# One top-k attention with two squared-ReLU FFNs: the last output weight is converted before the second input weight, one-tile units take two 128-blocks, and the order is written anew

## The chip, the cores and the metric

The kernel runs on one core of a Trainium2 chip. The metric is the device time of one execution in microseconds (us): the kernel before takes 1159.86 us, the median of three runs. TensorE is called PE here, VectorE DVE, ScalarE ACT, GpSimd POOL, and SyncE, which issues all the DMAs, SP.

## The reference

```python
scores = (q @ k.T) / sqrt(64)                 # 4 batches, 8 heads, 576 x 576
kth    = 32nd largest score of each row
attn   = softmax of the scores >= kth, 0 elsewhere
x      = (attn @ v), heads side by side       # 2304 tokens x 512
x      = (s * relu(x @ w_in)**2 + b) @ w_out        # moe: 512 -> 2048 -> 512
out    = relu(x @ w2_in)**2 @ w2_out                # moe2: 512 -> 2048 -> 512
```

The four weights arrive as 64-bit floats, which the kernel reads as pairs of 32-bit words; the rest is f32.

## The kernel before

**Tiles and units.** The 2304 tokens are 18 tiles of 128 rows. For each tile and head PE forms the scores into a PSUM bank pair `pS` (L599), DVE finds the 32nd largest in four rounds of `max` (L610) and three of `match_replace` (L621) and masks the exponentials (L652 or L658), ACT makes the exponential (L624) and its fp16 high half (L654 or L661), POOL the fp16 low half (L456, called from L673), a DMA transposes both into `pT` (L675), and PE multiplies by V into `pA` (L685). Eight heads make a tile of x; `finish_x` and `split_x` scale it, split it in two fp16 halves and transpose it by DMA into `xT` (L706).

**The FFNs.** `ffn(u, which)` runs a unit of one or two tiles through 16 blocks of 128 hidden columns. Per block: 12 matmuls into a PSUM bank (`f_in`, L788), a ReLU on ACT (L797), two squares on ACT (fp16 `gh`, L799, and f32 `gg`, L802), the low half `gl` on POOL (L807), then three matmuls per tile into `pC` (`f_out`, L834). The first FFN has units of one tile for tiles 0 to 10 and for tile 17, and three pairs; the second has one-tile units for tiles 0 and 17 and eight pairs. In one-tile units most blocks alternate between the banks `pH` and `pC[1]`; in pairs a block of 256 rows always uses `pH`. Before a second-FFN unit can start it needs its x in `xT[2]` or `xT[3]`, written by the end of the first FFN (`ffn1_end`, which adds the column sums `bcs`).

**The weights.** There are four, in 16 pieces each, numbered W0 (`moe_w_in`), W1 (`moe_w_out`), W2 (`moe2_w_in`), W3 (`moe2_w_out`). `pieces` loads a piece of 512 KB as pairs of words into a raw buffer, `to_f32` turns it into f32, `gram` takes its squared column norms on PE, `weight_scale` makes a power of two, and `split_w` makes two fp16 halves. Way D of `to_f32` uses three DVE operations (L919, L928, L935); way T gives the second to ACT (L924) and POOL (L456). Way P of `split_w` forms the low half on PE (two f32 passes L957 and one fp16 matmul L958, then a copy on ACT, L961); way O scales and rounds on ACT (L947, L948) and subtracts on POOL (L456). W0, W1 and W2 stay on chip (`w1`, `wo1`, `w2`). W3 is written back to DRAM as `wo2` (stores on SP) and streamed through the two `wring` buffers in each second-FFN unit. W0 and W1 use five raw buffers, W2 and W3 three; converted pieces of W3 wait in six f32 places, their halves in two staging tiles.

**The order.** Every operation is given to a planner (`Plan`) with a duration, a priority and the tiles it reads and writes; program order sets the dependences. `order()` simulates five engines and the DMA queue with these durations and with the delays of `WAIT`, picks by priority (`prio` plus an offset from the table `TW` by tag and by step), and its result is the fixed order in which each engine's instructions are emitted. An engine's instructions then run in that order whatever their real durations are. Before, the program order of the weights is W0, W1, the column sums (L1092), W2, W3.

Of the kernel before, what the change touches and what calls it, by code (L numbers as in the profile page):

```python
# [8 lines left out]
F32 = mybir.dt.float32  # L9
# [21 lines left out]
O2P = 10  # L31
O2S = 14
GROUPS = (1, 1, 4, 4)
CONV = ('DT', 'T', 'D', 'T')
SPLIT = ('P', 'P', 'O', 'P')
# [31 lines left out]
WKT = 2  # L67
# [45 lines left out]
}  # L113

WAIT = {("dve", "dve"): 0.127, ("act", "act"): 0.2, ("pool", "pool"): 0.1, ("pe", "pe"): 0.0, ("sp", "sp"): 0.0,
# [5 lines left out]
COLD, COLD_T = 1.35, 260.0  # L121
AVOID = 0.1
DMA_F, LAND, DRAIN = 1.3, 1.25, True
# [8 lines left out]
class Plan:  # L132
# [33 lines left out]
    def order(self):  # L166
# [27 lines left out]
        while len(out) < n:  # L194
# [59 lines left out]
            if kinds[i] == 2:  # L254
                end = max(end, queue if DRAIN else mine)
                queue = mine = (end if DRAIN else max(end, queue)) + lat
                done = queue + LAND
            elif kinds[i] == 1:
                queue = max(end + 0.65, queue) + lat * DMA_F
                if e == "sp":  # L260
                    mine = queue
                done = queue + LAND
# [21 lines left out]
def kernel(  # L284
# [81 lines left out]
    wraw += [(xT[i].rearrange("p a b -> p (a b)").bitcast(I32), [f"xT{i}_0", f"xT{i}_1"]) for i in range(3)]  # L366
# [200 lines left out]
    def attention(t, h, prio):  # L567
# [39 lines left out]
        for rd in range(TOPK // 8):  # L607
# [39 lines left out]
        else:  # L647
# [3 lines left out]
            if by_act:  # L651
                add(dve, "dv33", 0.65, prio, lambda: nc.vector.scalar_tensor_tensor(  # L652
# [4 lines left out]
            else:  # L657
                add(dve, "dv15", 0.73, prio, lambda: nc.vector.scalar_tensor_tensor(  # L658
# [63 lines left out]
    def finish_x(t, prio):  # L722
# [25 lines left out]
    nsub = [0]  # L748
    nring = [0]

    def ffn(u, which, prios):
        P.tag = f"F{which}{u}"
        nt = len(units[which][u])
        n = nt * 128
# [3 lines left out]
        x = xT[xt_i][:, :, x0 * 128:x0 * 128 + n]  # L758
        rx = [f"xT{xt_i}_{x0 + tt}" for tt in range(nt)]
        for f in range(KF):  # L760
# [4 lines left out]
            g1 = h2 if rdy else 0  # L765

            parts = "ab" if nt == 2 else "ab"[nsub[0] // 2 % 2]
            part3 = "ab" if nt == 2 else "ab"[nsub[0] // 3 % 2]
            if nt == 1:
                h2, g3 = nsub[0] % 2, nsub[0] % 3  # L770
                g1 = h2 if rdy else 0
                nsub[0] += 1
            o2 = 128 if parts == "b" else 0
            o3 = 128 if part3 == "b" else 0
            o1 = o2 if rdy else 0
            rrn = [f"rr{h2}{z}" for z in parts]
            ghn = [f"gh{g3}{z}" for z in part3]
            gln = [f"gl{g3}{z}" for z in part3]
            gn = [(("gg", "ggb"), ("sq", "dg"))[g1]["ab".index(z)] for z in (parts if rdy or nt == 2 else "a")]
            prio = prios[f]  # L780

            pin, pn_ = (pC[1], "pC1") if nt == 1 and h2 and rdy else (pH, "pH")

            def f_in(f=f, pin=pin):
                ps_ = pin[:, 0:n]
                for kk in range(KD):
                    for a, z in ((0, 0), (0, 1), (1, 0)):
                        nc.tensor.matmul(ps_, lhsT=win[:, f, a, kk, :], rhs=x[:, z * KD + kk, :],  # L788
                                         start=(kk == 0 and a == 0 and z == 0),
                                         stop=(kk == KD - 1 and a == 1))  # L790
# [345 lines left out]
    for t in range(NT):  # L1136
        prep_q(t, t * H - QP)
        for h in range(H):
# [8 lines left out]
            if t * H + h == WO2S >= H:  # L1147
                late_weights2()
# [41 lines left out]
```

## Time and profile before

| What | Value |
|---|---|
| runs | 1160.61, 1156.14, 1159.86 us |
| profiled execution: span from the first to the last instruction | 1163.6 us |
| busy: PE, DVE, ACT, POOL | 1033.9, 954.7, 884.4, 677.5 us |
| instructions | 27825 |
| DMA | 171.17 MB, mean 147 GB/s |

The page of the profile gives the busy time of each engine, the span in 40 slices, the chain of work that ended last and the costliest groups of instructions. Further views of the trace give busy times in chosen stretches, groups of instructions by line and shape with the idle time just before them, and the instructions in order of time. In the last, a bracket at the end of a row is the idle time of the engine before it and what ended it. A matmul's printed duration contains a part that overlaps the next one, so the pitch from start to start tells its cost.

### The profile page before, as it was taken

Reading aid. Unit: us, or ns where it says so; the run is one execution under the profiler, and the core shown is the slowest. Engines: PE = TensorE matmul, PEld = TensorE weight load, DVE = VectorE, ACT = ScalarE, POOL = GpSimd, SP = SyncE. Lnnn points to the kernel's source line nnn. Section 1 sums busy time; section 2 is a strip of 40 time slices with the busy share of each in tenths; the row PEclk is TensorE's granted clock in tenths of the full one; section 3 lists DMA queues with packets and bytes.
Section 4 is the critical chain, followed back from the end, with each engine's and each line's share of the span. In section 5 each row is a group of like instructions: output and inputs, shape, how many; then the busy total and the mean of one; then the engine's idle time right before and its main releaser. Section 6 shows DMA issues by size and latency. Waiting matters only on the chain. (4 is left out here: it accounts for less than half of the span.)

```text
span 1163.6 us, 27825 instructions
## 1 busy us (share of the span) xinstructions
PE 1033.9 (89%) x10052; PEld 693.2 (60%) x10052; DVE 954.7 (82%) x2034; ACT 884.4 (76%) x2354; POOL 677.5 (58%) x1109
## 2 busy tenths in 40 slices
PE   1476867689989999999999999999999999999998
PEld 1232344356667667666666776666666666666665
DVE  6999999999988999999999999987999999500000
ACT  3488869879889878879987899768777686564645
POOL 4676359766667756656775577646654474452322
PEclk9988989899999999999999999999999999999999
DMA  8888974676976774687588656765376277223530
GB/s 258 243 230 199 233 193 114 181 203 138 212 124 143 151 178 84 112 189 163 98 152 183 138 104 114 172 156 118 76 178 147 53 133 181 47 64 118 172 100 29
DMA packets 338219, 171.17 MB, mean 147 GB/s; under 512 B 292512, under 2 KB 317088, under 8 KB 338080
## 3 DMA queue, kind: packets, MB, share of 16 engines
q1 hardware_dynamic: 338080, 169.39, 62.9%
q8 instruction: 78, 1.28, 0.5%
q14 instruction: 61, 0.50, 0.2%
HBM read 89.65 MB, written 8.91 MB: 85 GB/s over the span
## 5 line engine op out<-in xcount | busy, mean ns | idle before, releaser
L788 PEld LDWEIGHTS <-w 128*128 128x128 f16 x4800 | 364.6, 98 | 87.7 <-issue 23.1
L788 PE MATMUL pH<-xT,w 128*128 128x256 f16 (+1 forms) x3648 | 368.2, 251 | 12.5 <-ACT rr L797 10.5
L456 POOL TENSOR_TENSOR pn<-et,pn 128x576 f16<-128x576 f32 x144 | 185.9, 1293 | 57.6 <-ACT pn L654 24.8
L797 ACT ACTIVATE rr<-pH,rsc 128x256 f32<-128x256 f32 (+1 forms) x304 | 128.8, 424 | 109.0 <-PE pH L788 107.0
L807 POOL TENSOR_TENSOR gl<-gg,gh 128x128 f16<-128x128 f32 (+1 forms) x216 | 114.4, 530 | 141.3 <-ACT gg L802 53.0
L610 DVE MAX8 m<-wk 128x8 f32<-128x576 f32 x252 | 188.9, 749 | 1.2
L834 PE MATMUL pC<-wo,gh 128*128 128x512 f16 x576 | 171.4, 379 | 0.0
L807 POOL TENSOR_TENSOR gl<-sqr,gh 128x128 f16<-128x128 f32 (+1 forms) x184 | 100.2, 545 | 115.6 <-ACT sqr L802 53.5
L834 PE MATMUL pC<-wring,gh 128*128 128x512 f16 x544 | 161.8, 379 | 1.7 <-DMA wring<-wo 1.1
L799 ACT ACTIVATE gh<-rr 128x128 f16<-128x128 f32 (+1 forms) x400 | 139.6, 352 | 8.2 <-PE pC L834 3.0
L834 PEld LDWEIGHTS <-gh 128*128 128x128 f16 x1152 | 103.0, 98 | 68.9 <-issue 2.3
L610 DVE MAX8 m<-spare 128x8 f32<-128x576 f32 x180 | 135.0, 750 | 0.6
L624 ACT ACTIVATE et<-pS,ngm,cq 128x576 f32<-128x576 f32 x144 | 119.0, 826 | 14.7 <-DVE wk L621 3.9
L621 DVE MATCH_REPLACE8 wk<-m,wk 128x576 f32<-128x576 f32 x168 | 124.8, 743 | 0.0
L610 DVE MAX8 m<-pS 128x8 f32<-128x576 f32 x144 | 108.2, 756 | 19.1 <-PE pS L599 18.7
L685 PEld LDWEIGHTS <-pT 128*128 128x128 f16 (+1 forms) x2400 | 85.8, 102 | 44.5 <-DMA pT<-pn 29.9
L834 PE MATMUL pC<-wo,gl 128*128 128x512 f16 x288 | 109.2, 379 | 2.8 <-POOL gl L807 2.8
L685 PE MATMUL pA<-vp,pT 128*128 128x64 f16 (+1 forms) x2400 | 95.0, 196 | 16.5 <-DMA pT<-pn 15.4
L834 PE MATMUL pC<-wring,gl 128*128 128x512 f16 x272 | 103.1, 379 | 0.0
L834 PEld LDWEIGHTS <-gl 128*128 128x128 f16 x576 | 56.3, 98 | 72.9 <-POOL gl L807 5.8
L599 PE MATMUL pS<-kT,qT 128*128 128x512 f16 (+2 forms) x320 | 84.4, 298 | 12.6 <-DVE et L652 10.3
L621 DVE MATCH_REPLACE8 spare<-m,spare 128x576 f32<-128x576 f32 x120 | 89.2, 743 | 0.0
(208 smaller groups left out, 1796.4 us busy)
## 6 DMA issues: line engine op xcount, KB each, us to landing
wring<-wo SPq DMA_DIRECT2D x72, 512.0 KB, 3.9
wring<-in_moe_w_out_dram SPq DMA_DIRECT2D x18, 512.0 KB, 3.8
wring<-in_moe_w_in_dram SPq DMA_DIRECT2D x17, 512.0 KB, 4.6
xT<-in_moe_w_in_dram SPq DMA_DIRECT2D x15, 512.0 KB, 5.8
xT<-in_moe_w_out_dram SPq DMA_DIRECT2D x14, 512.0 KB, 4.3
qW<-qT SPq DMA_DIRECT2D x36, 128.0 KB, 2.4
kvraw<-in_k_dram SPq DMA_DIRECT2D x16, 256.0 KB, 3.6
kvraw<-in_v_dram SPq DMA_DIRECT2D x16, 256.0 KB, 3.2
```

The source lines that it names most:

```text
L456: add(pool, step, c_pool(cols * (c.stop - c.start) / n), prio, lambda c=c: nc.gpsimd.tensor_tensor(o[:, c], x[:, c], y[:, c], op=op), r=r, ...
L599: nc.tensor.matmul(s[r0:r0 + n, c0:c0 + cn_], lhsT=w[:, h, r0:r0 + n], rhs=kk[:, k0:k0 + cn_], start=(a == 0), stop=(a == 1))
L610: add(dve, "dv10", 0.67, prio, lambda src=src, rd=rd: nc.vector.max(m[:, 8 * rd:8 * rd + 8], src), r=[sn], w=[f"m{i2}_{rd}"])
L621: add(dve, "dv11", 0.735, prio, lambda src=src, rd=rd: nc.vector.match_replace(wk, m[:, 8 * rd:8 * rd + 8], src, NEG), r=[sn, f"m{i2}_{rd} ...
L624: add(act, "ac9", 0.72, prio, lambda: nc.scalar.activation(out=e, in_=s, func=ACTF.Exp, bias=ngm[i2][:, 0:1], scale=cq[q2][:, j:j + 1]), r ...
L685: nc.tensor.matmul(pA[r0:r0 + n, h, :], lhsT=pT[p3][:, a * 5 + c, r0:r0 + n], rhs=vv[:, vc, z, :], start=(c == 0 and a == 0 and z == 0), s ...
L788: nc.tensor.matmul(ps_, lhsT=win[:, f, a, kk, :], rhs=x[:, z * KD + kk, :], start=(kk == 0 and a == 0 and z == 0), stop=(kk == KD - 1 and ...
L797: add(act, "ac18", 0.14 + n / 1200.0, prio, lambda r=r, pin=pin, rs=rs: nc.scalar.activation(out=r, in_=pin[:, 0:n], func=ACTF.Relu, scale ...
L799: add(act, "ac19", 0.094 + n / 1200.0, prio, lambda r=r, hi=hi: nc.scalar.activation(out=hi, in_=r, func=ACTF.Square), r=rrn, w=ghn)
L807: add(pool, "po19", 0.12 + n * 0.0021, prio, lambda gt=gt, hi=hi, lo=lo: nc.gpsimd.tensor_tensor(lo, gt, hi, op=ALU.subtract), r=gn + ghn, ...
L834: nc.tensor.matmul(pC[tt], lhsT=src[g3][:, c], rhs=wt(a), start=(f == 0 and a == 0 and src is gh), stop=(f == KF - 1 and src is gl))
```

## The change

Five things change. The program order of the weights becomes W0, W1, W3 with the column sums after W3's last scale, W2. The raw buffers become eight for W0, W1 and W3 (the two `wring`, `xT[2]`, `xT[3]` and four in the first half of `w2`) and four for W2; the f32 places of W3 are now eight, in the second half of `w2`, with five staging tiles; `xT[0]`, `xT[1]` and `spare` no longer serve the weights. W0 is converted in way D, W1 and W2 in D and T by turns, W3 in T as before; W3 is split in way O. A one-tile unit handles two blocks at once: 24 matmuls into the two halves of `pH`, then one ReLU, two squares and one subtraction over 256 columns, then six matmuls. The planner's table `TW` has new tags and new values throughout and some of its durations and delays change. New ways V, G and H are added in the code and not used.

```diff
-O2P = 10
-O2S = 14
+O2P = 1
+O2S = 6
-CONV = ('DT', 'T', 'D', 'T')
-SPLIT = ('P', 'P', 'O', 'P')
+CONV = ('D','DT','DT','T')
+SPLIT = ('P', 'P', 'O', 'O')
-WKT = 2
+WKT = -1
+RAWS = 8
+PD1 = (2, 3)
+CSW = (3, 15)
 TW = {
...
-WAIT = {("dve", "dve"): 0.127, ("act", "act"): 0.2, ("pool", "pool"): 0.1, ("pe", "pe"): 0.0, ("sp", "sp"): 0.0,
+WAIT = {("dve", "dve"): 0.2, ("act", "act"): 0.2, ("pool", "pool"): 0.1, ("pe", "pe"): 0.0, ("sp", "sp"): 0.0,
-COLD, COLD_T = 1.35, 260.0
+COLD, COLD_T = 2.0, 75.0
-DMA_F, LAND, DRAIN = 1.3, 1.25, True
+DMA_F, LAND, PRE, DRAIN = 1.1, 1.0, 1.0, True
-    wraw += [(xT[i].rearrange("p a b -> p (a b)").bitcast(I32), [f"xT{i}_0", f"xT{i}_1"]) for i in range(3)]
+    wraw += [(xT[i].rearrange("p a b -> p (a b)").bitcast(I32), [f"xT{i}_0", f"xT{i}_1"]) for i in (2, 3)]
+    wraw += [(w2[:, i:i + 2].rearrange("p c a k f -> p (c a k f)").bitcast(I32),
+              [f"w2{z}{c}" for c in (i, i + 1) for z in "shl"]) for i in range(0, RAWS, 2)]
-                add(dve, "dv11", 0.735, prio, lambda src=src, rd=rd: nc.vector.match_replace(
+                add(dve, "dv11", 0.66, prio, lambda src=src, rd=rd: nc.vector.match_replace(
-                add(dve, "dv33", 0.65, prio, lambda: nc.vector.scalar_tensor_tensor(
+                add(dve, "dv33", 0.725, prio, lambda: nc.vector.scalar_tensor_tensor(
...
-        for f in range(KF):
+        n, nf = 256, 2 // nt
+        for f in range(0, KF, nf):
...
-            pin, pn_ = (pC[1], "pC1") if nt == 1 and h2 and rdy else (pH, "pH")
+            fs = range(f, f + nf)
+            def f_in(fs=fs):
+                for j, ff in enumerate(fs):
+                    ps_ = pH[:, j * nt * 128:(j + 1) * nt * 128]
...
-            add(pe, "pe5", nt * 0.65, prio + 1.2, f_out, r=ghn + gln + rw,
+            add(pe, "pe5", 1.3, prio + 1.2, f_out, r=[*ghn, *gln, *rw],
...
-        i = wn[0] % 5 if wn[0] < 2 * KF else (0, 1, 3)[wn[0] % 3]
+        i = wn[0] % (len(wraw) if wn[0] < 3 * KF else 4)
...
+            if (wi, c) == CSW:
+                column_sums()
...
-    wsta = [x.bitcast(F32) for x in (alt[:, 0:2 * DM], alt[:, 2 * DM:], wstg_t, flat[0], flat[1])] + [spare]
+    wsta = [w2[:, c].rearrange("p a k f -> p (a k f)").bitcast(F32) for c in range(RAWS, KF)]
-    wstg = [kT[i][:, 0:2 * DM].rearrange("p (a f) -> p a f", a=2) for i in (4, 5)]
+    wstg = [x[:, 0:2 * DM] for x in (kT[4], kT[5], wstg_t)]
+    wstg += [vp[i].rearrange("p c a d -> p (c a d)")[:, 0:2 * DM] for i in (4, 5)]
...
     def late_weights():
-        pieces(2, moe2_w_in, w2, "w2", W2P, W2S, K_NORM, EXP_MASK, True)
+        ready2.append(1)
+        pieces(3, moe2_w_out, None, "wo2", O2P, O2S, K_HEAD - 1, FOUR_MASK, False)
+        pieces(2, moe2_w_in, w2, "w2", W2P, W2S, K_NORM, EXP_MASK, True)
...
-            column_sums()
             late_weights()
```

## Rows read from the trace of the kernel before

**Rows 1.** The page's busy times by engine and its PE line in 40 slices.
```profile
PE 1033.9 (89%) x10052; PEld 693.2 (60%) x10052; DVE 954.7 (82%) x2034; ACT 884.4 (76%) x2354; POOL 677.5 (58%) x1109
...
PE   1476867689989999999999999999999999999998
```

**Rows 2.** Stretches: PE, PEld, DVE, ACT, POOL busy; granted clock; DMA share; GB/s.
```profile
0.00:150.00 150.00, 87.63 (x459) 42.28 (x460) 139.28 (x271) 98.14 (x200) 82.21 (x100) 0.94 0.86 232
150.00:282.00 132.00, 99.57 (x1002) 63.41 (x1002) 129.59 (x279) 109.94 (x277) 95.86 (x139) 0.94 0.61 162
282.00:345.00 63.00, 56.42 (x726) 40.13 (x725) 56.98 (x123) 55.22 (x171) 42.24 (x73) 0.99 0.94 183
345.00:990.00 645.00, 624.68 (x6500) 434.32 (x6498) 609.13 (x1319) 525.75 (x1447) 399.13 (x690) 1.00 0.65 136
990.00:1164.00 174.00, 165.59 (x1377) 113.04 (x1374) 19.76 (x47) 95.35 (x261) 58.03 (x108) 1.00 0.29 89
```

**Rows 3.** PE in order of time, 225 to 235 us: two of W3's sixteen splits.
```profile
225.08 2.08 PE L957 MATMUL pC<-vp,gg 128*128 128x512 f32 x2 [0.97 <-DVE gg L998]
...
233.55 1.10 PE L957 MATMUL pC<-xT,gg 128*128 128x512 f32 x2
...
234.72 0.38 PE L599 MATMUL pS<-kT,qT 128*128 128x512 f16 x1
```

**Rows 4.** PE in order of time: FFN units' beginnings and ends between 148 and 343 us.
```profile
148.96 0.83 PE L788 MATMUL pH<-xT,w 128*128 128x128 f16 x12
...
228.35 1.47 PE L788 MATMUL pH<-xT,w 128*128 128x128 f16 x12
...
284.10 0.38 PE L834 MATMUL pC<-wo,gl 128*128 128x512 f16 x1
...
286.90 0.59 PE L834 MATMUL pC<-wring,gh 128*128 128x512 f16 x2
...
342.45 0.83 PE L788 MATMUL pH<-xT,w 128*128 128x128 f16 x12 [1.71 <-DMA xT<-xn]
```

**Rows 5.** SP in order of time: two loads of W3, tile 2's x, W3's last store.
```profile
179.85 0.33 SPq L417 DMA_DIRECT2D xT<-in_moe_w_out_dram  x1
...
213.04 0.33 SPq L417 DMA_DIRECT2D wring<-in_moe_w_out_dram  x1
...
282.01 1.23 SPq L706 DMA_TRANSPOSE xT<-xn  x1
283.34 0.53 SPq L417 DMA_DIRECT2D wo<-kT  x1
```

**Rows 6.** Groups by line and shape: busy, mean ns, then idle before and its releasers.
```profile
L788 PE MATMUL pH<-xT,w 128*128 128x256 f16 x2112 | 260.5, 273 | 3.2 <-ACT rr L797 3.1
L788 PE MATMUL pH<-xT,w 128*128 128x128 f16 x1536 | 107.7, 220 | 9.3 <-ACT rr L797 7.4 <-DMA xT<-xn 1.7
L797 ACT ACTIVATE rr<-pH,rsc 128x256 f32<-128x256 f32 x176 | 82.7, 470 | 98.2 <-PE pH L788 97.0 <-DVE ksa L487 0.6
L797 ACT ACTIVATE rr<-pH,rsc 128x128 f32<-128x128 f32 x128 | 46.1, 360 | 10.8 <-PE pH L788 9.9 <-DVE ksa L487 0.3
L456 POOL TENSOR_TENSOR w<-w 128x512 f16<-128x512 f32 x14 | 16.6, 1192 | 0.1
L928 DVE SCALAR_TENSOR_TENSOR w<-wring,w 128x512 int32<-128x512 int32 x12 | 10.2, 852 | 0.0
```

**Rows 7.** DVE's conversion line L919, one destination: duration ns min/median/max.
```profile
L919 DVE TENSOR_SCALAR wo<-xT x9: 407/414/1505, 50.8 to 88.0; 128x512 int32<-128x512 int32 x9
```

**Rows 8.** DVE in order of time, two interleaved heads at 501 and 507 us.
```profile
501.07 0.07 DVE L621 MATCH_VALUE_LOAD spare<-m,pS 128x8 f32 x1
...
501.80 0.08 DVE L621 MATCH_VALUE_LOAD wk<-m,wk 128x8 f32 x1
...
507.35 0.81 DVE L652 SCALAR_TENSOR_TENSOR et<-pS,m,et 128x576 f32<-128x576 f32 x1
508.07 0.75 DVE L610 MAX8 m<-spare 128x8 f32<-128x576 f32 x1
```

More of the change, by code (lines that the diff above doesn't have):

```diff
@@ L258, in order @@
             elif kinds[i] == 1:
-                queue = max(end + 0.65, queue) + lat * DMA_F
+                queue = max(end + PRE, queue) + lat * DMA_F
                 if e == "sp":
@@ L765, in ffn @@
             g1 = h2 if rdy else 0
[L767 to L777, printed above, removed]
@@ L778, in ffn @@
-            gln = [f"gl{g3}{z}" for z in part3]
-            gn = [(("gg", "ggb"), ("sq", "dg"))[g1]["ab".index(z)] for z in (parts if rdy or nt == 2 else "a")]
-            prio = prios[f]
-            pin, pn_ = (pC[1], "pC1") if nt == 1 and h2 and rdy else (pH, "pH")
[L784 to L790, printed above, removed]
@@ L792, in ffn @@
-            add(pe, "pe4", 12 * max(PEN, 0.0022 + n / 2400.0), prio, f_in,
-                r=rx + [f"{wname}h{f}", f"{wname}l{f}"], w=[pn_])
-            r, gt = rr[h2][:, o2:o2 + n], gg[g1][:, o1:o1 + n]
-            hi, lo = gh[g3][:, o3:o3 + n], gl[g3][:, o3:o3 + n]
+            rrn = [f"rr{h2}{z}" for z in "ab"]
+            ghn = [f"gh{g3}{z}" for z in "ab"]
+            gln = [f"gl{g3}{z}" for z in "ab"]
+            gn = [("gg", "ggb"), ("sq", "dg")][g1]
+            prio = prios[f]
+            fs = range(f, f + nf)
@@ new lines, in f_in @@
+            def f_in(fs=fs):
+                for j, ff in enumerate(fs):
+                    ps_ = pH[:, j * nt * 128:(j + 1) * nt * 128]
+                    for kk in range(KD):
+                        for a, z in ((0, 0), (0, 1), (1, 0)):
+                            nc.tensor.matmul(ps_, lhsT=win[:, ff, a, kk, :], rhs=x[:, z * KD + kk, :],
+                                             start=(kk == 0 and a == 0 and z == 0),
+                                             stop=(kk == KD - 1 and a == 1))
@@ L796, in ffn @@
+            add(pe, "pe4", 12 * nf * (0.0022 + 128 * nt / 2400.0), prio, f_in,
+                r=rx + [f"{wname}{z}{ff}" for ff in fs for z in "hl"], w=["pH"])
+            r, gt, hi, lo = rr[h2], gg[g1], gh[g3], gl[g3]
             rs = rsc[which][:, f * rsc[which].shape[1] // KF:][:, 0:1]
-            add(act, "ac18", 0.14 + n / 1200.0, prio, lambda r=r, pin=pin, rs=rs: nc.scalar.activation(
-                out=r, in_=pin[:, 0:n], func=ACTF.Relu, scale=rs), r=[pn_, f"rsc{which}"], w=rrn)
+            add(act, "ac18", 0.14 + n / 1200.0, prio, lambda r=r, rs=rs: nc.scalar.activation(
+                out=r, in_=pH[:, 0:n], func=ACTF.Relu, scale=rs), r=["pH", f"rsc{which}"], w=rrn)
@@ L807, in ffn @@
             add(pool, "po19", 0.12 + n * 0.0021, prio, lambda gt=gt, hi=hi, lo=lo: nc.gpsimd.tensor_tensor(
-                lo, gt, hi, op=ALU.subtract), r=gn + ghn, w=gln)
+                lo, gt, hi, op=ALU.subtract), r=[*gn, *ghn], w=gln)
             if which == 0:
-                rw = [f"wo1h{f}", f"wo1l{f}"]
-                wt = lambda a, f=f: wo1[:, f, a, :]
-            else:
-                if u >= len(units[1]) - LASTW:
-                    late = w1[:, f - f % 2:f - f % 2 + 2].rearrange("p f a k c -> p f a (k c)")
-                    rw = [f"w1{z}{f - f % 2 + i}" for z in "hl" for i in range(2)]
-                    if f % 2 == 0 and u == len(units[1]) - LASTW:
-                        add(sp, "sp15", 0.47, prio - LWP, lambda late=late, f=f: dma(late, wo2[f // 2]),
-                            r=[f"wo2_{f}", f"wo2_{f + 1}"], w=rw, lat=1.46)
-                    wt = lambda a, f=f, late=late: late[:, f % 2, a, :]
-                elif f % 2 == 0:
+                rw = [f"wo1{z}{ff}" for ff in fs for z in "hl"]
+                wt = lambda a, ff: wo1[:, ff, a, :]
+            elif u >= len(units[1]) - LASTW:
+                late = w1[:, f - f % 2:f - f % 2 + 2].rearrange("p f a k c -> p f a (k c)")
+                rw = [f"w1{z}{f - f % 2 + i}" for z in "hl" for i in range(2)]
+                if f % 2 == 0 and u == len(units[1]) - LASTW:
+                    add(sp, "sp15", 0.47, prio - LWP, lambda late=late, f=f: dma(late, wo2[f // 2]),
+                        r=[f"wo2_{f}", f"wo2_{f + 1}"], w=rw, lat=1.46)
+                wt = lambda a, ff, late=late: late[:, ff % 2, a, :]
+            else:
+                if f % 2 == 0:
                     ri = nring[0] % NWR
@@ L825, in ffn, with f_out @@
                         r=[f"wo2_{f}", f"wo2_{f + 1}"], w=[f"ring{ri}"], lat=1.46)
-                if u < len(units[1]) - LASTW:
-                    rw = [f"ring{ri}"]
-                    wt = lambda a, f=f, ri=ri: wring[ri][:, f % 2, a, :]
-            def f_out(f=f, g3=g3, wt=wt, o3=o3):
-                for tt in range(nt):
-                    c = slice(o3 + tt * 128, o3 + tt * 128 + 128)
+                rw = [f"ring{ri}"]
+                wt = lambda a, ff, ri=ri: wring[ri][:, ff % 2, a, :]
+            def f_out(fs=fs, g3=g3, wt=wt):
+                for j, (ff, tt) in enumerate([(ff, tt) for ff in fs for tt in range(nt)]):
+                    c = slice(j * 128, j * 128 + 128)
                     for src, a in ((gh, 0), (gh, 1), (gl, 0)):
-                        nc.tensor.matmul(pC[tt], lhsT=src[g3][:, c], rhs=wt(a),
-                                         start=(f == 0 and a == 0 and src is gh),
-                                         stop=(f == KF - 1 and src is gl))
-            add(pe, "pe5", nt * 0.65, prio + 1.2, f_out, r=ghn + gln + rw,
+                        nc.tensor.matmul(pC[tt], lhsT=src[g3][:, c], rhs=wt(a, ff),
+                                         start=(ff == 0 and a == 0 and src is gh),
+                                         stop=(ff == KF - 1 and src is gl))
+            add(pe, "pe5", 1.3, prio + 1.2, f_out, r=[*ghn, *gln, *rw],
                 w=[f"pC{tt}" for tt in range(nt)])
@@ L905, in place, with to_f32 @@
         return dst[:, c].rearrange("p a k f -> p (a k f)" if len(dst.shape) == 5 else "p a f -> p (a f)").bitcast(F32), [f"{nm}s{c}"]
[L907 to L909 removed]
+    def to_f32(src_ap, o, on, prio, shape, way):
+        i = wn[0] % (len(wraw) if wn[0] < 3 * KF else 4)
         wn[0] += 1
@@ L945, in split_w @@
         way = SPLIT[wi][c % len(SPLIT[wi])]
-        if way == "O":
+        if way in "HG":
+            if way == "G":
+                add(dve, "dv34", 0.335, prio, lambda: nc.vector.tensor_scalar(o, o, sc, None, op0=ALU.mult), r=[scn], w=on, lock=True)
+                add(dve, "dv35", 0.335, prio, lambda: nc.vector.tensor_scalar(hi, o, 1.0, None, op0=ALU.mult), r=on, w=hn, lock=True)
+            else:
+                add(dve, "dv35", 0.335, prio, lambda: nc.vector.tensor_scalar(hi, o, sc, None, op0=ALU.mult), r=on + [scn], w=hn, lock=True)
+        elif way == "O":
             add(act, "ac25", 0.61, prio, lambda: nc.scalar.activation(out=o, in_=o, func=ACTF.Copy, scale=sc), r=[scn], w=on)
@@ L950, in split_w @@
             add(act, "ac27", 0.62, prio, lambda: nc.scalar.activation(out=hi, in_=o, func=ACTF.Copy, scale=sc), r=on + [scn], w=hn)
-        if way == "P":
-            pd, pdn = (pC[1], ["pC1"]) if wi > 1 else (pH, ["pH", "pY"]) if nsp[0] % 2 else (pC[0], ["pC0"])
-            d = 1 if wi > 1 else j % 2
+        if way in "PH":
+            pd, pdn = (pC[1], ["pC1"]) if wi in PD1 else (pH, ["pH", "pY"]) if nsp[0] % 2 else (pC[0], ["pC0"])
+            d = 1 if wi in PD1 else j % 2
             nsp[0] += 1
@@ L995, in weight_scale @@
                   [f"wsm{wi}_{j}"], f"wsi{wi}_{j}", f"wsc{wi}_{j}", f"wsv{wi}_{j}", mask=mask)
-        if "P" in SPLIT[wi]:
-            d = 1 if wi > 1 else j % 2
+        if "P" in SPLIT[wi] or "H" in SPLIT[wi]:
+            d = 1 if wi in PD1 else j % 2
             add(dve, "dv25", 0.2, prio, lambda: nc.vector.tensor_scalar(
@@ L1026, in pieces @@
                     continue
-                w_s = [f"{nm}s{x}"] if x > 1 else []
+                w_s = [f"{nm}s{x}"]
                 hi, lo = (dst[:, x, a].rearrange("p k f -> p (k f)") if inward else dst[:, x, a] for a in range(2))
```

54 lines of the change are left out of this document (27 added, 27 removed), and 80 rows, old and new, of the table TW.

## Prediction

> **What bounds the kernel now.** I read the page first, then the busy times by stretch, then PE in order of time, then the groups by line with the idle time before them.
>
> The page has PE busy for 1033.9 us of a span of 1163.6 [rows 1]; its line of slices is thin at the left and full from the tenth slice on. By stretches [rows 2] the 130 us in which PE is idle lie so: 62.4 in the first 150 us (150 - 87.6), 32.4 from 150 to 282 us, 6.6 to 345, 20.3 in the 645 us to 990, 8.4 at the end. DVE is the other full engine: 139.3 of 150, 129.6 of 132, 609.1 of 645 us, and nearly nothing after 990. So the early part is set by DVE, which does conversions and attention at once, and from 282 us on PE is full and stays full for 170 us after DVE has ended. What PE needn't do, or can do before 282 us instead of after, comes off the end; what only moves inside the early part doesn't.
>
> In the early part the first FFN of tile 0 starts at 148.96, that of tile 1 at 228.35, and the latter's last matmul is at 284.10 [rows 4], though a one-tile unit is 16 blocks of about 1.3 us, 21 us. The second FFN of tile 0 has its first output matmul at 286.90; the last store of W3 is issued at 283.34 and tile 2's x at 282.01 [rows 5]. At 342.45 PE waits for tile 3's x [rows 4].
>
> **The change part by part.** The sums go by the profiled execution; its span of 1163.6 us is 3.7 above the median of the runs, 1159.9, and I carry differences over to the median.
>
> *W3's split leaves PE.* A split costs PE two f32 passes and one fp16 matmul: from start to start 1.17 us (233.55 to 234.72); where PE had idled before, the two passes took 2.08 us instead of 1.10 [rows 3]. Sixteen at 1.17 are 18.7 us; one or two slow ones make it 20; I take 19. They lie at 205 to 280 us, where PE has idle time as well, so nothing is won unless other work takes their place. This work exists: with 19 us less between its blocks, tile 1's first FFN ends about 260 instead of 284, and tile 0's second FFN, 21 us, can go before tile 2's x arrives at 286. It needs W3 in DRAM and W2 split by then. Today W3's last store is at 283.34; W2 comes last now, but W3 and W2 have more places to land in, and the stretch to 150 us already moves 232 GB/s [rows 2]. POOL's work is the check. From 100 us on W3 and W2 need 24 additions and 32 subtractions of 1.2 us, 67 us. The rest of POOL's work is, from 150 to 282 us, 95.9 less W2's 16 subtractions and W3's 16 additions, so 57 of 132 us, and some 69 of the 160 us from 100 to 260. Together 136 of 160 us: it fits, without much room. Between 0 and -19 I take -19, because tile 0's unit fills the gap by itself.
>
> *The wait at 342 us.* With PE ahead, tile 3's x may be waited for as before, but the pair of tiles 1 and 2 is now there to run. Bounds 0 and -5; I take -2.
>
> *Two blocks in one.* Of 224 one-tile blocks 112 pairs are made. Matmuls stay the same in number and size. ACT's ReLU costs 470 ns for 256 columns against 360 for 128 [rows 6], so 250 ns less for two; with the two squares about 650 ns less, 73 us of ACT in all. ACT has 525.8 of 645 us busy [rows 2], so this is no time by itself; it counts where PE waits for ACT. PE's idle time before one-tile input matmuls on the ReLU is 7.4 us for those in `pH` [rows 6]; for 176 blocks of 256 columns, already with one bank, it is 3.1, which for 112 is 2. So -5. If the cover is gone, that is, if an input comes right behind an input without an output between, each costs about 0.5 us: at most 112 times, +56, but the 176 blocks show that such orders are rare. Range +10 to -7. The last unit has fewer, longer steps at its end: +1.
>
> *Conversions.* Way D instead of T in 8 pieces of W0 and 8 of W1, T instead of D in 8 of W2: 8 more of DVE's second operation (L928), 852 ns each [rows 6], +6.8 us on an engine with 99% in that stretch. In exchange ACT and POOL lose 8 operations each. x of every tile comes up to 6.8 us later; PE is full from 282 us on and hides most of it. Between 0 and 6.8 I take +2, nearer to 0 since PE has a unit more to do at that time.
>
> *W3's subtraction on POOL.* Sixteen of 1.19 us [rows 6], 19 us more there, against 8 additions fewer and 21 us saved in the FFN blocks. POOL is busy 95.9 of 132 us [rows 2]: cost nothing, covered by its idle time.
>
> DVE's conversion operation takes 414 ns as a rule and up to 1505 [rows 7], which shows that it can be held. The Trainium skill (GPSIMD Engine Reference, Specifications) says that GpSimd shares its SBUF interfaces with VectorE, so that an operation with two SBUF inputs is slowed; by that rule sixteen more subtractions would hold sixteen conversions by at most 1.1 us, +17 on DVE before 282 us. The net number of long POOL operations in the weights, however, rises by only 8 (minus 8 in W0, 8 in W1, plus 8 in W2, 16 in W3), so by the rule it is about +9. The sum here doesn't hold it.
>
> *Column sums after W3.* Tile 0's x for the second FFN waits for `bcs`, and for `xT[2]`, a raw buffer of W2 now. PE's queue isn't held, since tile 1's unit needs only `pC[0]`, which is emptied ahead of both. Nothing is lost until tile 2's first FFN is done, about 307 us; each us after that costs one. I take 0, upper bound +10.
>
> *The order.* All priorities are new, so each queue (PE, DVE, ACT, POOL and SP) has another order. What can be priced are the durations given to the planner. For `match_replace` it now has 0.66 us; the trace has 0.73 from the start of its load to the next (501.07 to 501.80) [rows 8]. For the masking it has 0.725 instead of 0.65, and the trace has 0.72 (507.35 to 508.07). A head so comes out 0.22 us too short (3 x 0.07 and little else), against 0.08 before; over 144 heads 31 us against 11. PE runs in the planned order and meets heads that aren't ready. Some of this is in the 20.3 us of idle time of rows 2. Cost 0 to +31; I take +5, because FFN matmuls stand between two heads and the delay `WAIT` of DVE on itself rises from 0.127 to 0.2, which gives back a part where heads don't interleave.
>
> Sum: -19 - 2 - 5 + 1 + 2 + 5 = -18, and 1159.9 - 18 = 1142 us.
>
> **The rivals.** *Order behind reality (slower).* The planner's short DVE price passes on in full: PE's attention matmuls stand too early in its queue and the FFN matmuls behind them wait. 31 us less the 19 won and with the other terms at -2 - 5 + 1 + 2 = -4 makes 1160 - 19 - 4 + 31 = 1168. For it: DVE is busy 609 of 645 us, with 36 us of slack. Against it: the order of before had 11 us of the same error and PE still lost only 20.3 us. It decides from a loss of some 23 us on, that is when PE's idle time from 345 to 990 us passes 43 us.
>
> *The freed time stays idle.* W2 is ready only at 285 us or later, as W3 was, and tile 0's second FFN doesn't come forward: PE's busy time falls by 19 us and its idle time before 282 us rises by 19. 1160 - 5 + 1 + 2 + 5 = 1163, with -2 for 342 us about 1161. For it: DVE, at 98%, must do 8 operations more by then. Against it: between 179.85 and 213.04 us no piece of W3 was loaded [rows 5], for lack of places; that hole closes.
>
> *More than the split.* With weights done by 230 us and 73 us less ACT work the new order also takes half of the 20.3 us from 345 to 990 and the rest of the 6.6 us before: 1142 - 10 - 5 = 1127, and without the +5 for the order 1122. For it: ACT and POOL are relieved just where both stretches of one-tile units lie. Against it: no row shows that the 20.3 us are waits for ACT; the 7.4 us before one-tile matmuls are in the forecast already.
>
> **How the numbers follow.** Forecast 0.48, its own range 1130 to 1152; more than the split 0.18; freed time idle 0.18; order behind reality 0.16. About 0.5%, 5.8 us here, is what a measurement of this kernel can tell from no change. Faster by more than that (under 1154): the forecast, the larger gain, and a little of the idle case, 0.68. Within 0.5% (1154 to 1166): most of the idle case, and a half-way order, 0.17. Slower: most of the order case, 0.15. The range 1120 to 1167 leaves out about 2 in 10: half of the order case, a part of the larger gain's lower end, and orders worse than any priced here.
>
> **What would show it.** Right: no L957 matmul of W3, PE's busy time about 1010 us; the second FFN of tile 0 on PE before 282 us; ACT busy near 805 us; idle time before 256-column input matmuls on the ReLU still a few us; PE idle from 345 to 990 us at most 25 us. Wrong: first output matmul from `wring` after 285 us with more idle time ahead of it (freed time idle); waits of PE for `pT` or for DVE's masking well above 25 us after 345 us (order); ReLU waits of tens of us (two blocks in one). PE at its lower level for long stretches before 282 us would eat a part too: at 225 us, after waits, W3's passes took 2.08 us against 1.10 at 233 [rows 3].
>
> The granted clock from 150 to 282 us is 0.94 of full speed in the mean [rows 2]. The Trainium skill (TensorE: Matmul & The Clock Gate, Part 1) has PE throttled by default and released by activity, so a PE with 19 us less to do there could be at the lower level longer; that work lies in idle time and would change the sum by little, so no term stands for it.

## The result, and the profile after

The changed kernel takes 1149.72 us (median of five runs, 1147.30 to 1152.27); the kernel before took 1160.61 beside it. The ratio is 0.9908 with a 95% interval from 0.9878 to 0.9937, so the change saves 10.9 us (7.3 to 14.2). The forecast was 1142, with 1130 to 1152 as its own range.

Stages are compared by the two profiled executions: spans 1163.6 before and 1145.7 after. The former lies 3.0 us above 1160.61 and the latter 4.0 us below 1149.72, so their difference is 17.9 us instead of 10.9; some 7 us of what follows is spread between single executions, not the change. The page of the changed kernel, busy times and PE line:

```profile
PE 1012.4 (88%) x10004; PEld 689.0 (60%) x10004; DVE 949.9 (83%) x2038; ACT 841.6 (73%) x2010; POOL 672.4 (59%) x1005
...
PE   2157768677899999999999999999999999999998
```

The changed kernel by stretches, columns as in [rows 2]; the last two rows are the same time cut once at 345 us:

```profile
0.00:150.00 150.00, 70.75 (x442) 38.96 (x442) 137.88 (x291) 93.94 (x195) 84.15 (x105) 0.95 0.90 252
150.00:282.00 132.00, 101.95 (x1012) 66.90 (x1012) 130.27 (x277) 105.86 (x230) 104.75 (x128) 0.87 0.59 151
282.00:345.00 63.00, 57.26 (x771) 41.55 (x769) 58.31 (x120) 52.24 (x128) 42.88 (x59) 1.00 0.74 169
345.00:990.00 645.00, 630.68 (x6548) 437.33 (x6546) 619.39 (x1339) 510.81 (x1266) 391.48 (x630) 1.00 0.64 137
...
0.00:345.00 345.00, 229.96 (x2219) 147.41 (x2220) 326.46 (x686) 252.03 (x551) 231.79 (x291) 0.93 0.75 198
345.00:1166.00 821.00, 782.46 (x7789) 541.55 (x7786) 623.41 (x1352) 589.61 (x1460) 440.56 (x715) 1.00 0.56 125
```

The kernel before, cut in the same way at 345 us, and its stretch from 200 to 282 us, for an experiment below:

```profile
0.00:345.00 345.00, 243.63 (x2185) 145.82 (x2187) 325.85 (x671) 263.30 (x647) 220.31 (x311) 0.95 0.78 196
345.00:1166.00 821.00, 790.26 (x7874) 547.37 (x7871) 628.88 (x1365) 621.10 (x1708) 457.16 (x798) 0.99 0.57 126
200.00:282.00 82.00, 63.62 (x588) 38.23 (x588) 80.13 (x176) 67.39 (x168) 54.12 (x85) 0.94 0.62 168
```

Read the two cuts together. Up to 345 us PE is busy for 13.7 us less (243.6 to 230.0), though W3's splits alone took 18.7: the freed time turned for the most part into idle time. After 345 us PE has 7.8 us less left to do (790.3 to 782.5, 85 matmuls fewer): up to 345 us it has done some 40 more FFN input matmuls (832 weight loads against 792) and some 40 more with V (600 against 557), and as many FFN output matmuls as before (192). And from 345 us to the end of the span it is idle for 18.2 us instead of 28.3 (1145.7 - 345 - 782.5; 1163.6 - 345 - 790.3). These two, 7.8 and 10.1, are the 17.9; at any cut the two would sum to the difference of the spans.

What PE waits for from 345 us on (total us, times, longest), before:

```profile
PE pA L685 <- DMA pT<-pn: 11.1, 14, 2.6
PE pH L788 <- ACT rr L797: 8.6, 16, 1.0
PE pC L788 <- ACT rr L797: 1.3, 2, 0.7
```

and after:

```profile
PE pA L692 <- DMA pT<-pn: 6.2, 10, 1.2
PE pH L784 <- ACT rr L792: 3.9, 7, 0.9
```

The waits for the ReLU (`rr`) fall from 9.9 to 3.9 us, those for the transposed probabilities from 11.1 to 6.2.

The places that the forecast named, changed kernel in order of time, all engines:

```profile
174.03 2.72 PE L784 MATMUL pH<-xT,w 128*128 128x128 f16 x24 [1.15 <-ACT wo L969]
...
201.76 7.07 PE L1103 MATMUL pC<-wo,ones 128*128 128x512 f16 x32 [0.75 <-DVE wsm L1000]
...
263.08 1.24 SPq L713 DMA_TRANSPOSE xT<-xn  x1
...
272.52 1.50 PE L784 MATMUL pH<-xT,w 128*128 128x128 f16 x24
...
277.96 0.38 PE L828 MATMUL pC<-wo,gl 128*128 128x512 f16 x1
...
279.83 0.20 POOL L1071 TENSOR_TENSOR rsc<-wrt,wsv 128x4 f32<-128x4 f32 x1
...
280.08 0.47 ACT L792 ACTIVATE rr<-pH,rsc 128x256 f32<-128x256 f32 x1
...
280.60 1.50 PE L784 MATMUL pH<-xT,w 128*128 128x128 f16 x24 [0.56 <-ACT rr L792]
...
281.06 1.33 ACT L955 ACTIVATE kT<-kT,wsc 128x512 f32<-128x512 f32 x2
...
285.21 2.27 POOL L463 TENSOR_TENSOR w<-kT,w 128x512 f16<-128x512 f32 x2
...
288.37 0.59 PE L828 MATMUL pC<-wring,gh 128*128 128x512 f16 x2
```

The first FFN of tile 0 starts at 174.03, not at 148.96 as in [rows 4]: W1's splits are now on PE until 170 us, and DVE has done more of attention ahead of them (48 `max` up to 150 us, 42 before). Tile 1's first FFN ends at 277.96 (before: 284.10). The second FFN of tile 0 has its first input at 272.52: a one-tile unit now has eight inputs of 24 matmuls, tile 0's first FFN those from 174.03 to 199.24, tile 1's those from 234.46 to 265.92, and the one at 272.52 is the next. Its second input is only at 280.60 and its first output at 288.37 (before: 286.90). Its x was sent on its way at 263.08; what came last was W2. The ReLU behind the first input is scaled by `rsc`, which needs the scales of all four groups of W2; `rsc` is written at 279.83 and that ReLU starts at 280.08. W2's last scaling on ACT is at 281.06, its last subtraction on POOL at 285.21.

Groups of the changed kernel by line and shape, columns as in [rows 6]:

```profile
L784 PE MATMUL pH<-xT,w 128*128 128x256 f16 x2112 | 259.4, 273 | 3.5 <-ACT rr L792 3.3 <-DMA xT<-xn 0.2
L784 PE MATMUL pH<-xT,w 128*128 128x128 f16 x2688 | 172.3, 222 | 6.4 <-ACT rr L792 5.1 <-ACT wo L969 1.1
L792 ACT ACTIVATE rr<-pH,rsc 128x256 f32<-128x256 f32 x288 | 134.7, 468 | 131.6 <-PE pH L784 131.0
```

All 288 ReLUs have 256 columns at 468 ns, as [rows 6] had it for that shape. The one-tile input matmuls wait for them for 5.1 us in the whole execution, 4.6 of these up to 345 us. Before, those in `pH` waited for 7.4 us [rows 6] and those in `pC` for 1.3:

```profile
L788 PE MATMUL pC<-xT,w 128*128 128x128 f16 x1152 | 80.3, 220 | 2.5 <-ACT rr L797 1.3 <-ACT xs L882 0.9
```

### The profile page after: what moved, and what is told of

The parts are those of the page before. It is cut to its first block, busy times and chain, and to the rows that moved or that the text cites. A ratio compares the mean times of both kernels' runs of the same rounds, so it can differ in the third digit from the quotient of the medians.

```text
span 1145.7 us, 27208 instructions
## 1 busy us (share of the span) xinstructions
PE 1012.4 (88%) x10004; PEld 689.0 (60%) x10004; DVE 949.9 (83%) x2038; ACT 841.6 (73%) x2010; POOL 672.4 (59%) x1005
## 4 chain that ended last, share of the span: by engine, by line
PE 40%; DVE 30%; DMA 6%; issue 4%; ACT 3%; POOL 3%; SPq 0%; POOLq 0%; DVEq 0%; ACTq 0%
PE pH L784 18%; PE pC L828 17%; DVE m L617 13%; DVE wk L628 5%; DVE spare L628 5%; DMA pT<-pn 4%; DVE et L659 3%; PE pA L692 3%; PE pS L606 2%; DVE w L937 1%; POOL pn L463 1%; POOL gl L802 1%; DVE et L665 1%; ACT et L631 1%; POOL knat L463 1%
## 5 line engine op out<-in xcount | busy, mean ns | idle before, releaser
L784 PE MATMUL pH<-xT,w 128*128 128x128 f16 (+1 forms) x4800 | 431.7, 244 | 9.9 <-ACT rr L792 8.5
L792 ACT ACTIVATE rr<-pH,rsc 128x256 f32<-128x256 f32 x288 | 134.7, 468 | 131.6 <-PE pH L784 131.0
L463 POOL TENSOR_TENSOR pn<-et,pn 128x576 f16<-128x576 f32 x144 | 186.8, 1300 | 66.5 <-ACT pn L661 33.1
L802 POOL TENSOR_TENSOR gl<-gg,gh 128x256 f16<-128x256 f32 x152 | 103.4, 680 | 111.6 <-ACT gh L794 85.0
L617 DVE MAX8 m<-spare 128x8 f32<-128x576 f32 x216 | 162.2, 751 | 0.7
L617 DVE MAX8 m<-wk 128x8 f32<-128x576 f32 x216 | 161.9, 749 | 0.9
L802 POOL TENSOR_TENSOR gl<-sqr,gh 128x256 f16<-128x256 f32 x136 | 91.3, 671 | 110.9 <-ACT gh L794 82.9
L794 ACT ACTIVATE gh<-rr 128x256 f16<-128x256 f32 x288 | 116.1, 405 | 2.3 <-PE pC L828 1.1
L692 PE MATMUL pA<-vp,pT 128*128 128x64 f16 (+1 forms) x2400 | 95.0, 196 | 17.9 <-DMA pT<-pn 17.4
L628 DVE MATCH_REPLACE8 spare<-m,spare 128x576 f32<-128x576 f32 x144 | 107.2, 744 | 0.0
L628 DVE MATCH_REPLACE8 wk<-m,wk 128x576 f32<-128x576 f32 x144 | 107.1, 744 | 0.0
```

The source lines that it names most:

```text
L463: add(pool, step, c_pool(cols * (c.stop - c.start) / n), prio, lambda c=c: nc.gpsimd.tensor_tensor(o[:, c], x[:, c], y[:, c], op=op), r=r, ...
L617: add(dve, "dv10", 0.67, prio, lambda src=src, rd=rd: nc.vector.max(m[:, 8 * rd:8 * rd + 8], src), r=[sn], w=[f"m{i2}_{rd}"])
L628: add(dve, "dv11", 0.66, prio, lambda src=src, rd=rd: nc.vector.match_replace(wk, m[:, 8 * rd:8 * rd + 8], src, NEG), r=[sn, f"m{i2}_{rd}" ...
L692: nc.tensor.matmul(pA[r0:r0 + n, h, :], lhsT=pT[p3][:, a * 5 + c, r0:r0 + n], rhs=vv[:, vc, z, :], start=(c == 0 and a == 0 and z == 0), s ...
L784: nc.tensor.matmul(ps_, lhsT=win[:, ff, a, kk, :], rhs=x[:, z * KD + kk, :], start=(kk == 0 and a == 0 and z == 0), stop=(kk == KD - 1 and ...
L792: add(act, "ac18", 0.14 + n / 1200.0, prio, lambda r=r, rs=rs: nc.scalar.activation(out=r, in_=pH[:, 0:n], func=ACTF.Relu, scale=rs), r=[" ...
```

## The experiments

Three theories. A: PE gains because ACT and POOL have less to do per one-tile block. B: the gain is W3's split, which leaves PE. C: part of both is lost again in the new order of the queues. Experiments of a first kind keep every queue's order as the planner wrote it and change only what one instruction does. Those of a second kind change the program and let the planner make a new order.

**Two blocks issued as four halves (A).** The changed kernel, its order kept.

```diff
-            add(act, "ac18", ..., lambda r=r, rs=rs: nc.scalar.activation(
-                out=r, in_=pH[:, 0:n], func=ACTF.Relu, scale=rs), ...)
+            cs = [slice(0, 256)] if nt == 2 else [slice(0, 128), slice(128, 256)]
+            add(act, "ac18", ..., lambda r=r, rs=rs, cs=cs: [nc.scalar.activation(
+                out=r[:, c], in_=pH[:, c], func=ACTF.Relu, scale=rs) for c in cs], ...)
```

The two squares and the subtraction likewise. 

> The changed kernel with every instruction in the same place, but in one-tile units the ReLU, the two squares and the subtraction are each issued as two halves of 128 columns, as before the change: 336 more ACT instructions and 112 more on POOL, by the rows of before some 73 us more of ACT and 21 us more of POOL. Theory A (the gain is that PE waits less after 345 us since ACT has less to do per one-tile block): 6 to 12 us slower than the changed kernel, most of it between 345 and 990 us. Theory B (the gain is W3's split leaving PE): within 3 us of the changed kernel. Theory C (the gain is the new order): within 3 us as well, as the order is the same.

Measured: 1158.15 us, ratio to before 0.9971 (0.9956 to 0.9987), so 7 us above the changed kernel (about 4 either way). Its stretches up to 345 us and from there:

```profile
0.00:345.00 345.00, 223.94 (x2172) 142.12 (x2173) 324.28 (x684) 257.50 (x641) 234.13 (x319) 0.94 0.75 196
345.00:1166.00 821.00, 786.99 (x7833) 544.63 (x7831) 626.63 (x1355) 612.66 (x1707) 456.17 (x799) 1.00 0.57 126
```

A's size is met. Its place is met by half: PE has 4.5 us more left to do at 345 us (787.0 against 782.5) and is idle 4.6 us longer afterwards (1154.8 - 345 - 787.0 = 22.8 against 18.2). Up to 345 us PE waits for ACT longer at two places, for the ReLU by 2.6 us (7.2 against 4.6) and for the squares of K and V by 2.8 (14.9 against 12.1). After 345 us its wait for the ReLU is 2.0 us longer than the 3.9 of the changed kernel:

```profile
PE pH L784 <- ACT rr L793: 5.9, 12, 0.7
```

That is a third of the 6.0 us by which this wait fell. The halves do not bring back the second bank or the order of before, so what made the rest of it fall isn't shown.

**Six more matmuls a group (B).** The changed kernel, its order kept; f32, 256 columns, behind the last squared norm of each of the eight groups of W3 and W2, 22 us of PE.

```diff
+            if wi >= 2 and c % per == per - 1:
+                for _ in range(6):
+                    nc.tensor.matmul(pC[1][:, 128:384], lhsT=ones32, rhs=o[:, 0:256], start=True, stop=True)
```

> The changed kernel in the same order, with PE work given back early: the last gram of each of the eight groups of W3 and W2 is followed by six more f32 matmuls of 256 columns whose output nobody reads, about 22 us of PE at full clock, spread between 100 and 255 us. Theory A (PE time in that stretch is idle anyway): less than 5 us slower than the changed kernel. Theory B (the freed 19 us are what was won): 15 to 22 us slower. Theory C says nothing on it.

Measured: 1167.58 us, ratio 1.0052 (1.0034 to 1.0071), 17 us above the changed kernel (about 4 either way). PE after 345 us:

```profile
345.00:1166.00 821.00, 797.81 (x7978) 552.91 (x7972) 636.06 (x1377) 600.29 (x1489) 450.98 (x728) 1.00 0.57 127
```

None of the added matmuls lies there, yet 15.3 us more work is left (797.8 against 782.5). B's number is met, but not by B's mechanism. What DVE waits for up to 345 us:

```profile
DVE sqr L999 <- PE pC L992: 16.5, 8, 3.5
```

The added matmuls stand ahead of DVE's reading of the squared norms, in the same bank, and DVE waits for them each of the eight times, 16.5 us in all (in the changed kernel it waits there once, 0.3 us). DVE, which sets the early part, does 17.7 us less up to 345 us (308.8 against 326.5). So the 17 us are what DVE lost, and the experiment doesn't tell what PE's early time is worth by itself. The expectation of the next experiment still takes it as evidence for B.

**W3's f32 passes left out of the kernel before (B, the other way round).** The order before is kept.

```diff
-                nc.tensor.matmul(pd, lhsT=dgs[d], rhs=o, start=True, stop=False)
-                nc.tensor.matmul(pd, lhsT=minus, rhs=hi, start=False, stop=True)
+                if wi != 3:
+                    nc.tensor.matmul(pd, lhsT=dgs[d], rhs=o, start=True, stop=False)
+                nc.tensor.matmul(pd, lhsT=minus, rhs=hi, start=(wi == 3), stop=True)
```

> The kernel before in its own order; in the 16 splits of W3 TensorE's two f32 passes are left out, only the fp16 matmul of 0.23 us stays (so the low half of W3 in this output is not the weight's). That takes 16 x 0.94 = 15 us off TensorE between 205 and 280 us and changes no queue otherwise. Theory B (TensorE's early work counts one for one or nearly so, as six added matmuls a group showed with +17 of 22): 1160 - 10 to 1160 - 15, that is 1145 to 1150. Rival (in the order of before this work lies in idle time, and it was the new order that made use of it): 1157 to 1161.

Measured: 1153.94 us beside 1162.07, ratio 0.9941 (0.9920 to 0.9962): 6.9 us less (4.4 to 9.3) for 15 us taken out. Neither answer: a little under half comes through. Its stretches:

```profile
0.00:345.00 345.00, 238.26 (x2235) 147.14 (x2236) 328.08 (x678) 266.11 (x657) 222.68 (x315) 0.88 0.76 196
345.00:1166.00 821.00, 782.32 (x7787) 542.63 (x7785) 625.06 (x1357) 618.25 (x1699) 455.30 (x795) 1.00 0.57 126
200.00:282.00 82.00, 54.76 (x566) 36.35 (x564) 80.72 (x176) 67.99 (x169) 54.93 (x86) 0.83 0.66 171
```

After 345 us PE has 7.9 us less left (790.3 to 782.3). The changed kernel has 782.5, which looks the same; but the spans of these two profiles, 1163.6 and 1150.9, lie 12.7 us apart where the runs lie 6.9 apart, so some 6 us of the difference is spread between executions. From 200 to 282 us, where the passes stood, its busy time falls by 8.9 of the 15 us and becomes idle time; it does only 10 matmuls more there (566 against 588 - 32), at a granted clock of 0.83 instead of 0.94.

**Fewer conversions on DVE.** The changed kernel, its order kept.

```diff
+                k = 1 if wn[0] - 1 in few else DM
                 add(dve, "dv20", 0.602, prio, lambda: nc.vector.scalar_tensor_tensor(
-                    oi, lo, 29, oi, op0=ALU.logical_shift_right, op1=ALU.bitwise_or), ...)
+                    oi[:, 0:k], lo[:, 0:k], 29, oi[:, 0:k], op0=..., op1=...), ...)
```

> The changed kernel in its own order; the second conversion operation on VectorE (128x512, some 0.8 us) is cut to one column in 8 pieces of W0 and 8 of W1, those that went by ScalarE and GpSimd in the kernel before (the lowest bits of these weights are left out). 16 x about 0.75 = 12 us less on VectorE before 175 us. Theory that the conversions are the mis-sized term: the first FFN of tile 0 starts 6 to 12 us earlier and the time falls by 5 to 10 us, to 1140 to 1145. Rival (forecast: what lies on VectorE there is hidden by full TensorE later, 2 us at most): 1147 to 1150. Rival (the order puts attention ahead, so that FFN work doesn't come forward): start earlier by under 3 us and no gain.

Measured: 1147.36 us, ratio to before 0.9873 (0.9849 to 0.9896), 4 us under the changed kernel, give or take 4. That is between the answers and isn't told from zero. Tile 0's first FFN doesn't start earlier, as the last rival had it. Part of the time saved on DVE goes into waits for loads, 5.3 and 3.7 us up to 175 us, where the changed kernel has 4.5 and none; up to 345 us DVE is busy for 4.9 us less (321.6 against 326.5), not 12.

```profile
174.49 2.72 PE L784 MATMUL pH<-xT,w 128*128 128x128 f16 x24 [1.15 <-ACT wo L972]
```

```profile
DVE w L925 <- DMA wring<-in_moe_w_in_dram: 5.3, 3, 3.9
DVE w L925 <- DMA w<-in_moe_w_in_dram: 3.7, 2, 2.3
```

So in this order the conversions' duration isn't what makes the start late. That the order does is the explanation left, and not shown by itself.

**The change in steps, each with a new order (C).** The kernel before with W3 split in way O; then with the two-block units as well; then with the new places and program order as well, under the table of before:

```diff
-SPLIT = ('P', 'P', 'O', 'P')
+SPLIT = ('P', 'P', 'O', 'O')
```

> The kernel before with one edit: W3 is split on ACT and POOL (way O) instead of PE; table, durations and the places are those of before, and the planner makes a new order of it. PE busy about 20 us less. Theory A: within 4 us of the kernel before, PE's idle time before 282 us up by as much as its work falls. Theory B: 12 to 20 us faster than before. Theory C: anywhere within 10 us of before, for reasons of order.

> The kernel before with W3 in way O and with one-tile units of two 128-blocks; table, durations and places of before. ACT busy about 72 us less. Theory A: 6 to 12 us faster than the kernel with way O alone, the gain after 345 us. Theory B: within 4 us of the kernel with way O alone. Theory C: anywhere within 10 us of it.

> The kernel before with W3 in way O, two-block one-tile units, and the weights' new places and program order (eight raw buffers, W3 ahead of W2, column sums after W3's last scale); table, conversions and durations of before. Weights loaded and converted earlier than in the kernel without the new places. Theory A: within 4 us of the two-block kernel, since what is early is idle anyway. The forecast's view (the second FFN of tile 0 comes forward before 282 us): 8 to 15 us faster than the two-block kernel. Theory C: anywhere within 10 us.

Measured: 1174.34, 1176.69 and 1190.12 us, ratios 1.0116 (1.0093 to 1.0139), 1.0134 (1.0114 to 1.0153) and 1.0262 (1.0238 to 1.0285): all slower than before. The first lies outside all three answers, the second within 4 us of the first, the third 13 us above the second and again outside all answers. Taken alone the first would say that W3's split does harm, the opposite of the nearest edit in a kept order. What a new order costs by itself has to be known first.

**The changed kernel with the planner's durations and delays of before.**

```diff
-                add(dve, "dv11", 0.66, prio, ...)
+                add(dve, "dv11", 0.735, prio, ...)
```

with `WAIT`, `COLD`, `DMA_F`, `LAND`, `PRE`, two more durations of DVE, three of ACT and one of POOL. 

> The changed kernel with the planner's durations and delays of before (match_replace 0.735, masking 0.65, the delays of DVE on itself and of DMA, the cold factor), the new table kept. If the short price of match_replace costs time, as the forecast held with 5 us: 3 to 10 us faster than the changed kernel. If the table fits only the durations with which it stands: 3 to 15 us slower. Theory A: as the changed kernel, within 4 us.

Measured: 1175.32 us, ratio 1.0141 (1.0114 to 1.0167). With the price of `match_replace` that is nearer to the trace (0.735; 0.73 in [rows 8]) and the other old values the kernel is slower by 26 us, more than any of the answers.

**Noise on the priorities.** Both kernels with up to half a unit on each operation's priority, a unit being the step from one head to the next in the order; then both with a second draw (500 in place of 1).

```diff
+        prio += ((n * 7919 + 1) % 997) / 997.0 - 0.5
```

> The changed kernel with up to 0.5 added to or taken from every operation's priority, by its number: the same work, another order. It measures what the choice of the order alone does. Theory C: 5 to 15 us slower or faster than the changed kernel. Theory A: within 4 us.

> The kernel before with the same small changes of its priorities: the same work, another order. Theory C: 5 to 15 us from the kernel before. Theory A: within 4 us of it.

> The changed kernel with another draw of the same noise of half a unit on each priority. With the first draw it took 1173.7, the kernel before 1189.0. Theory that an order which is not fitted costs either kernel 20 to 30 us and that the changed work itself is worth some 15: 1168 to 1180, and 10 to 20 below the kernel before with the same draw. Rival (single orders differ by more than that, and the 15 was one draw's luck): a difference to the kernel before under 5 or over 25.

> The kernel before with that second draw of noise. Theory: 1180 to 1195, 10 to 20 above the changed kernel with the same draw. Rival (one draw's luck): a difference under 5 or over 25.

| Draw | changed kernel | kernel before |
|---|---|---|
| none | 1149.72 | 1160.61 |
| first | 1173.70 (ratio 1.0118, 1.0095 to 1.0140) | 1188.95 (1.0250, 1.0228 to 1.0273) |
| second | 1190.46 (1.0244, 1.0222 to 1.0265) | 1186.04 (1.0222, 1.0199 to 1.0245) |

Noise alone costs 24 to 41 us, more than the 15 us that theory C allowed, and the changed kernel's two draws lie 17 us apart. After the first draw I held the difference of 15 us to be what the changed work is worth without a fitted order. With the second draw the changed kernel is 4 us above the kernel before, and the two intervals overlap: that theory falls. The steps above and the old durations (1174 to 1190) all lie in the same band, and nothing on a single part can be read from them. The changed kernel in the first draw's order (first row) and in the second's (in the next fence), 345 us to the end:

```profile
345.00:1200.00 855.00, 805.67 (x8081) 558.03 (x8078) 641.94 (x1390) 612.53 (x1500) 455.42 (x733) 1.00 0.55 123
```

```profile
345.00:1200.00 855.00, 801.90 (x7921) 555.48 (x7918) 632.04 (x1365) 606.36 (x1481) 448.98 (x725) 0.98 0.54 122
```

In both PE has some 20 us more to do after 345 us than in the fitted order (805.7 and 801.9 against 782.5).

## Why the prediction was right, and where it was not

**The bound.** Right as far as the profiles tell: from 345 us on PE is busy for all but 18.2 us of 800.7 (before: 28.3 of 818.6), so what counts is how much PE has left at 345 us and how little it waits from there on. That DVE sets the early part agrees with the added matmuls: 16.5 us of waits on DVE came out as 17 us.

**W3's split, -19.** Right in sign, too large by about half, and this is the mis-sized term. In the order of before 15 us less brought 6.9; at that rate 18.7 would make 8.6 us (18.7 x 6.9 / 15). This is an estimate: in the changed kernel's own order the split was not measured apart. The step that failed is "I take -19, because tile 0's unit fills the gap by itself". The unit did not come forward: of its inputs only the first, at 272.52, lies far ahead of 282 us, and its first output is at 288.37, in the place that the forecast had named as the sign of freed time gone idle. Tile 1's first FFN, forecast to end at about 260, ends at 278. The unit waits for W2, as the rival "the freed time stays idle" had it, though not for its halves but for its scales: the first ReLU can't start before `rsc`, at 279.83. The rival itself gave 1161, and is wrong as a whole: some 40 FFN input matmuls and as many with V, done by 345 us, filled part of the gap. That the time still lies in the forecast's range is in part luck, since what its largest term rested on did not happen.

**Two blocks in one, -5.** Right in size: to issue the halves again costs 7 us, within 4. The forecast placed it in the waits for the ReLU before one-tile inputs, 7.4 us to 2. They fall from 8.7 (with those in `pC`) to 5.1 in the whole execution, 4.6 of these early, and the halves bring them to 9.5. From 345 us on they fall by 6.0 us, of which the halves bring back only a third. Not foreseen was that half of what the halves cost comes before 345 us.

**ACT near 805 us.** Wrong: 841.6. The forecast took 73 us off ACT's busy time for the FFN and some 5 for conversions. The groups do give that: ReLUs and squares sum to 442.3 us before (163.4, 139.6 and 139.3, of the three lines) and 369.8 after (134.7, 116.1 and 119.0), 72.5 less. But neighbouring instructions of ACT overlap in the rows, and the engine's busy time counts an overlap once: all groups of ACT together sum to 1058.8 us before and 974.7 after, 84.1 less, and its busy time fell by 42.8 (884.4 to 841.6). A difference of groups is no difference of busy time.

**The wait at 342 us, -2; the last unit, +1; conversions, +2; column sums, 0; W3's subtraction on POOL, 0.** No experiment has them apart, except that 16 operations less on DVE gave 4 us, uncertain by 4: +2 for 8 more isn't contradicted. In the two profiles PE's waits for x fall from 1.7 us to 0.2. POOL took its new work without a rise: 672.4 us busy, 677.5 before. The column sums are on PE for 7 us from 201.76, and x for the second FFN is sent 9 us ahead of the first input (263.08 to 272.52), whose ReLU then waits for `rsc`: nothing lost there.

**The order, +5.** Its price can't be measured apart, as the noise shows. By difference: -8.6 and -7 leave +5 of the measured -10.9 for all that remains, where the forecast's terms sum to +6 (-2 + 1 + 2 + 5). That they agree is arithmetic with an uncertainty of some 6 us, and the two shares come from different orders, so they needn't add up. How much of the 10.9 us is a better or worse fitted order stays open. The rival "order behind reality" is answered: from 345 to 990 us PE idles for 14.3 us (645 - 630.7), where that case wanted 43. Early, PE idles for 79 us up to 150 us (62 before), and tile 0's first FFN starts 25 us later; what that costs in the end was not measured.

**"More than the split", 1122.** Its mechanism is seen, PE's idle time from 345 to 990 us falling from 20.3 to 14.3; its size is not.

## What to carry to other kernels

Work taken off an engine that is half idle in that stretch is neither free nor worth its duration: take it out in the kept order and see what is left to do where the engine becomes full; here a little under half came through. Work put in to test an engine's idle time must stand where nobody waits for it: look at the waits of the other engines before reading the time. In a kernel whose queues are written out by a planner with a fitted table, change what an instruction does and keep the order: a new order, even from half a unit of noise, moved the time by two to four times the whole effect, and a second draw took away the difference that the first had shown. Take an engine's saving from its busy time, not from the sum of its groups.

## What the runs showed of the hardware

With fewer matmuls, PE was slower for those left. Without W3's f32 passes the granted clock from 200 to 282 us was 0.83 instead of 0.94 (the mean over its two levels, 1.2 and 2.4 GHz). The rows show it too: the same matmul of the scores in the kernel before (first row) and without the passes (second).

```profile
207.28 0.38 PE L599 MATMUL pS<-kT,qW 128*128 128x512 f16 x1
206.38 0.63 PE L599 MATMUL pS<-kT,qW 128*128 128x512 f16 x1
```

In the changed kernel 24 input matmuls took 2.72 us at 174.03, after a stretch with much waiting, but 1.50 at 280.60. The durations in the rows are the safer sign: from 25 to 75 us, where the edit changes nothing, the two profiles give 0.99 and 0.66 as the granted clock, while such a matmul takes 0.63 us in both at 29 us. The forecast had said that a lower clock would change the sum by little; in the kernel without the passes it can be one of the reasons why 15 us freed brought so few matmuls forward before 282 us, and its share was not measured apart. The Trainium skill (TensorE: Matmul & The Clock Gate, Part 1) has the clock throttled by default and released by activity; the trace agrees.

DVE's conversions didn't become slower with W3's subtractions on POOL. The second operation can't tell, since 24 of its 32 lie before 90 us and the first of these subtractions is at 119.5. The third (L935, after L937) can: from 150 to 282 us it took 800 ns in the mean before (14.40 us for 18) and 762 after (16.01 us for 21), while POOL's two-input line (L456, after L463) was busy for 63.7 and 74.0 us. The Trainium skill (GPSIMD Engine Reference, Specifications) has GpSimd's SBUF interfaces shared with VectorE; the +9 us that the forecast weighed by it isn't seen as a rise here.
